# The first weight loads of a fused FFT filter and gated MLP: gate in quarters over two queues, up in halves

## The chip, the cores and the metric

The kernel runs on one core of one Trainium2 chip. The metric is the time of one execution on the device, in microseconds (us), median over several runs. A core has five engines that work side by side and meet through semaphores: TensorE (PE in the profile; its weight loads are PEld), VectorE (DVE), ScalarE (ACT), GpSimd (POOL) and SyncE (SP). Each takes its instructions in order. Transfers between main memory (HBM) and the core's memory (SBUF) are issued by one of these engines, as an instruction in its queue, and carried out by 16 DMA engines.

## The reference

Two branches work on the same normalized input, and both are added to the input. `A` filters the whole 2048 x 512 array by a two-dimensional FFT; `B` is a gated MLP with hidden width 1792.

```python
def _A_ref(x, w_r, w_i):
    X = rfft2(x.astype(float32), axes=(-2, -1))
    y = irfft2(X * (w_r + 1j * w_i), s=(S, D)).astype(bfloat16)
    return y

def _B_ref(x, w_gate, w_up, w_down):
    g = jnp.einsum("bsd,df->bsf", x, w_gate)
    u = jnp.einsum("bsd,df->bsf", x, w_up)
    h = _gelu(g) * u                      # tanh form
    return jnp.einsum("bsf,fd->bsd", h, w_down)

x = A_x                                   # 1 x 2048 x 512, bfloat16
xn = _layernorm(x, axis=-1)
return x + _A_ref(xn, A_w_r, A_w_i) + _B_ref(xn, B_w_gate, B_w_up, B_w_down)
```

## The kernel before

The 2048 rows are 16 chunks `c` of 128 rows (row 16p + c lies on partition p of chunk c). Everything is in bfloat16, with 32-bit sums in PSUM.

**Layer norm.** Of each chunk VectorE takes the statistics (L339, L342); the root of the variance comes from ScalarE for chunks 0 and 1 (L394) and from GpSimd for the others (L357, L361). The normalized chunk `xn` is needed with the contraction on the partitions: for chunks 0 to 3 TensorE transposes it (L351, four 128 x 128 transposes each) and a copy brings it to `xnT`, for chunks 4 to 15 a transposing DMA of SyncE does (L455).

**The MLP.** The contraction of 512 is four blocks `e` of 128 (`NE`), and the weight tiles `Wg_sb` and `Wu_sb` hold `[128, e, 1792]`. A unit of work (`unit`, L470) is a gate product into `g_ps`, an up product into `u_ps`, the GELU on ScalarE (`ge`, L503) and the product on VectorE (`hT`, L508). At first units are small: chunk 0 alone with the first 512 hidden columns, chunk 1 with the same columns, chunks 0 and 1 with columns 512 to 767 and 768 to 1023, then chunks 2 and 3; from hidden column 1024 on a unit takes four chunks. The gate product of the very first unit is cut in two (`mm_half`, L493): first all columns for e = 0 and 1, then for e = 2 and 3. All other products run column block by column block, each over all four e. Later come the down products (L817).

**The FFT.** It is matmuls with tables (`RF`, `CT`), folds on VectorE, a filter multiply and the way back, spread between the MLP's units. Three rows of indices, `idx_t`, serve the gathers of the filter (L594), which GpSimd issues from about 43 us on.

**What sets the order.** A small planner (`Plan`, L135) simulates five engines with estimated durations and writes out each engine's instructions in the order that results. It takes, in order of `key`, the operation that can start first. The arrival of loads is given to it as constants: `LAND` for x, `WG_LAND` and `WU_LAND` for the gate and up columns (L308 to L311), for example

```python
WG_LAND = [6.3] * 4 + [10.2] * 4 + [13.2] * 6
WU_LAND = [7.4] * 4 + [11.7] * 4 + [15.2] * 6
```

They shape the order alone; on the chip each instruction waits for its data. The order on each engine is fixed, so an operation whose data is late holds up all that stands behind it on its engine.

**The opening.** Ahead of the planned part stand the memsets (VectorE: `spin`, `eps_t`, `minus_half`), a warming square root on ScalarE (L280) that loads its table, 37 small matmuls on zeros (`spin`, L320) that keep TensorE at work until the first transposes, six more behind those (`spin_on`, L322), and all opening loads, in SyncE's queue, in the order of the code: x chunk 0, x chunk 1, the indices, gate and up columns 0 to 511, x 2 and 3, gate and up 512 to 1023, x 4 to 7, gate and up 1024 to 1791, x 8 to 11, `RF`, x 12 to 15, tables, filter. The loads' completions are counted on a ring of semaphores, and an issue that comes round to one still in use waits for it.

Of the kernel before, what the change touches and what calls it, by code (L numbers as in the profile page):

```python
# [10 lines left out]
P = 128  # L11
# [3 lines left out]
ALU = mybir.AluOpType  # L15
AF = mybir.ActivationFunctionType
# [3 lines left out]
NC = 16  # L20
NG = 8
NE = 4
DF = 1792
# [178 lines left out]
def kernel(  # L202
# [45 lines left out]
    def load_consts(first, last):  # L248
        a, b = ccols[first][0], sum(ccols[last])
        nc.sync.dma_start(out=CT[:, a:b], in_=cap[:, a:b])  # L250


    def load_x(c0, n, eng=nc.sync):
        eng.dma_start(out=x_t[:, c0:c0 + n, :], in_=x_v[:, c0:c0 + n, :])

    def load_w(a, b, eng=nc.sync):
        nc.sync.dma_start(out=Wg_sb[:, :, a:b], in_=wg_v[:, :, a:b])
        eng.dma_start(out=Wu_sb[:, :, a:b], in_=wu_v[:, :, a:b])
# [1 line left out]
    eps_t = pc.tile([P, 1], F32, name="eps_t")  # L260
    spin = pc.tile([P, P], BF16, name="spin")
    warm = pc.tile([P, 1], F32, name="warm")
    nc.vector.memset(spin[:], 0.0)
    nc.vector.memset(eps_t[:], EPS)
    minus_half = pc.tile([P, 4], F32, name="minus_half")
    nc.vector.memset(minus_half[:], -0.5)
    ident_t = pc.tile([P, P], BF16, name="ident_t")
    nc.gpsimd.memset(ident_t[:], 1.0)
    nc.gpsimd.affine_select(out=ident_t[:], in_=ident_t[:], pattern=[[-1, P]], compare_op=ALU.is_equal, fill=0.0,
                            base=0, channel_multiplier=1)  # L270

    def load_x(c0, n, eng=nc.sync):
        return eng.dma_start(out=x_t[:, c0:c0 + n, :], in_=x_v[:, c0:c0 + n, :])  # L273

# [1 line left out]
        v = wg_v if T is Wg_sb else wu_v  # L276
        return eng.dma_start(out=T[:, e, a:b], in_=v[:, e, a:b])  # L277

    pin = tc.keep_in_program_order
    pin(nc.scalar.activation(out=warm[:], in_=eps_t[:], func=AF.Sqrt, bias=eps_t[:], scale=1.0))  # L280
    pin(load_x(0, 1))
    pin(load_x(1, 1))
    idx_t = pc.tile([P, 3], I32, name="idx_t")
    nc.sync.dma_start(out=idx_t[:], in_=nc.inline_tensor(idx_np, name="spec_rows").ap())  # L284
    load_w(Wg_sb, 0, 512)
    load_w(Wu_sb, 0, 512)
    load_x(2, 2)
    load_w(Wg_sb, 512, 1024)
    load_w(Wu_sb, 512, 1024)
    load_x(4, 2)  # L290
    load_x(6, 2)
    load_w(Wg_sb, 1024, DF)
    load_w(Wu_sb, 1024, DF)
    load_x(8, 2)
    load_x(10, 2)
    for c in range(0, NC, 8):
        nc.sync.dma_start(out=RF_t[:, c:c + 8], in_=rf_d.rearrange("p (c k) -> p c k", c=NC)[:, c:c + 8])
    load_x(12, 2)
    load_x(14, 2)
    load_consts("F0", "L0")  # L300
    load_consts("I0", "M0")
    for T, w_in in ((TR, A_w_r), (TI, A_w_i)):
        rows = w_in.rearrange("(kb a h g) k -> h kb a (g k)", kb=NC, h=2, a=8)
        Tf = T.rearrange("p j k -> p (j k)")
        for h in range(2):
            nc.sync.dma_start(out=Tf[64 * h:64 * h + 64, W:8 * W], in_=rows[h, :, 0:4, W:8 * W])

    LAND = {0: 2.9, 1: 3.6, 2: 8.4, 3: 8.4}  # L308
    LAND.update({c: 11.5 if c < 8 else 17.5 if c < 12 else 20.5 for c in range(4, NC)})
    WG_LAND = [6.3] * 4 + [10.2] * 4 + [13.2] * 6  # L310
    WU_LAND = [7.4] * 4 + [11.7] * 4 + [15.2] * 6  # L311
    RF_LAND = 19.0

    ident = ident_t[:]
# [1 line left out]
    IQ = [cc(f"I{q}") for q in range(4)]  # L316

    sp_ps = ps.tile([P, D], F32, name="sp_ps", tag="S", bufs=4)
    for k in range(37):
        pin(nc.tensor.matmul(sp_ps[:, :P], lhsT=spin[:], rhs=spin[:], start=True, stop=True))  # L320

    def spin_on():  # L322
        for k in range(6):
            nc.tensor.matmul(sp_ps[:, :P], lhsT=spin[:], rhs=x_t[:, 0, :P], start=True, stop=True)
# [12 lines left out]
    def f_stats(c):  # L337
        tiles["st", c] = st = pw.tile([P, V.BN_STATS_DIM], F32, name="stats", bufs=4)
        V.bn_stats(out=st[:], in_=x_t[:, c, :])  # L339
# [34 lines left out]
    def first_two():  # L374
# [50 lines left out]
        o["copyt"].rel = ("S",)  # L425
        xT_op[1] = o["copyt"]
        xn_op[1] = o["xn1"]

    ROOT = 1.1
    first_two()  # L430

    def moments(c, key):
        s = add("DVE", 0.6, lambda: f_stats(c), key=key, t_min=LAND[c] if c < 4 else max(LAND[c], 14.7))
        return add("DVE", 0.1, lambda: f_mean(c), [s], key=key - 0.5)

    def second_two():
        m = [moments(c, -1200 + c) for c in (2, 3)]
        m = add("POOL", ROOT, lambda: root_eps(2, 2), m, key=-1190, lat=ROOT + 0.1)
        for c in (2, 3):
            xn_op[c] = add("DVE", 0.33, lambda c=c: f_norm_v(c, 0, D), [m], key=-1180 + c, lat=0.53)  # L440
            t = add("PE", 0.23, lambda c=c: f_T(c, 0, NE), [xn_op[c]], key=-880 + c, lat=0.5, acq=("S",))
            e, f = ("ACT", A.copy) if c == 2 else ("DVE", V.tensor_copy)
            xT_op[c] = add(e, 0.5, lambda c=c, f=f: f_Tc(c, 0, NE, f), [t], key=-1100 + c, rel=("S",))
# [26 lines left out]
    def unit(k, c0, n, f0, m=1):  # L470
# [50 lines left out]
            g = add("PE", occ / 2, lambda: mm_half(1), [xT_op[0], g], key=1000.1, lat=occ / 2 + 0.3)  # L521
        else:
            g = split("g_ps", "G", Wg_sb, 1000 + k, WG_LAND, m)
        u = split("u_ps", "U", Wu_sb, 1003.1 if k == 2 else 1000.5 + k, WU_LAND, (2, m, 1)[k] if k < 3 else m)
        ge = add("ACT", {1: 0.28, 2: 0.36, 4: 0.5}[n * m], f_ge, [g], key=-1000 + k,
                 lat={1: 0.38, 2: 0.48, 4: 0.7}[n * m], acq=("ge",), rel=("G",))
        h = add("DVE", {1: 0.21, 2: 0.34, 4: 0.61}[n * m], f_h, [ge, u], key=-1000 + k, rel=("U", "ge"))
# [318 lines left out]

    E_ = mybir.EngineType
    with tc.manual_schedule(engines={E_.PE, E_.DVE, E_.Activation, E_.Pool, E_.SP}):
        for op in plan.order():
            op.fn()  # L850

# [29 lines left out]
```

## Time and profile before

| | us |
|---|---|
| median of 6 runs | 178.6 (178.43 to 178.74) |
| the profiled execution | 179.56 |
| its span, first to last instruction | 177.9 (177.855) |
| TensorE busy | 172.5 |
| VectorE, ScalarE, GpSimd busy | 116.0, 95.9, 17.2 |
| first gate block: issued, landed | 2.17, 7.3 |
| first up block: issued, landed | 2.65, 8.75 |
| x chunks 2 and 3: issued, landed | 3.20, 9.5 |
| second gate block: issued, landed | 3.75, 10.95 |
| second up block: issued, landed | 4.22, 12.4 |

The profile is of one execution, which here was longer than each of the six runs. "Busy" is the time in which an engine had an instruction under way. A row of a timeline gives start, duration, engine, line and operation, the tile written and those read, and in brackets the idle time before it with what ended it. The chain of waits starts at the last instruction and goes back from each to what released it, so it shows what the end of the kernel hung on. In a row by windows, each engine's busy time in that stretch is followed by the granted TensorE clock (1.00 is full), the mean busy share of the DMA engines and the GB/s they moved.

### The profile page before, as it was taken

The numbers are of one execution on the slowest core, as the hardware profiler recorded it, in microseconds if no ns is written. First come the engines' busy times: TensorE is split into PE (matmuls) and PEld (weight loads), VectorE is DVE, ScalarE is ACT, GpSimd is POOL, SyncE is SP. The second block draws the span as 40 slices with busy tenths as digits, with TensorE's granted clock in tenths as the row PEclk, the third lists the DMA queues.
The fourth block names the chain that finished last, engine by engine and source line by source line (L and its number), as shares of the span: only waits on it lengthen the run. The fifth ranks groups of instructions, "written<-read, shape, count | busy, mean of one in ns | idle before, by whom it ended". The sixth has DMA issues, their size and how long they took to land.

```text
span 177.9 us, 3132 instructions
## 1 busy us (share of the span) xinstructions
PE 172.5 (97%) x1145; PEld 96.7 (54%) x1145; DVE 116.0 (65%) x255; ACT 95.9 (54%) x170; POOL 17.2 (10%) x38
## 2 busy tenths in 40 slices
PE   7699999999999999999999999999999999999993
PEld 7599845455545544555555445454444445444563
DVE  3487999987443598979899999634525334344233
ACT  4433398899735888898899974453112111211200
POOL 1020322504761000000000000000000000000000
PEclk9999999999999999999999999999999999999999
DMA  4999996424725902112201420200132222222212
GB/s 89 352 372 379 368 199 109 88 59 65 215 81 178 355 1 59 46 28 50 58 14 48 121 68 24 54 5 4 42 105 87 64 88 61 88 83 65 75 47 59
DMA packets 21871, 19.35 MB, mean 109 GB/s; under 512 B 8480, under 2 KB 20000, under 8 KB 21856
## 3 DMA queue, kind: packets, MB, share of 16 engines
q1 hardware_dynamic: 21440, 17.84, 35.1%
q0 software_dynamic: 416, 1.32, 2.5%
q8 instruction: 9, 0.15, 0.4%
q14 instruction: 6, 0.05, 0.1%
HBM read 13.38 MB, written 2.10 MB: 87 GB/s over the span
## 4 chain that ended last, share of the span: by engine, by line
PE 94%; DMA 3%; SPq 1%; issue 0%; DVE 0%
PE u_ps L490 27%; PE y_ps L817 27%; PE g_ps L490 27%; DMA Wu_sb<-in_B_w_up_dram 3%; PE gp L738 2%; PE bp L577 2%; PE yp L768 2%; PE dp L635 2%; PE y_ps L821 2%; PE ep L644 2%; SPq L273 0%; PE tp L351 0%; SPq L277 0%; SPq L284 0%; DVE y_sb L824 0%
## 5 line engine op out<-in xcount | busy, mean ns | idle before, releaser
L490 PE MATMUL u_ps<-xnT,Wu_sb 128*128 128x512 bf16 (+2 forms) x272 | 57.3, 341 | 0.2 <-DMA Wu_sb<-in_B_w_up_dram 0.2
L490 PE MATMUL g_ps<-xnT,Wg_sb 128*128 128x512 bf16 (+2 forms) x256 | 56.2, 349 | 0.0
L817 PE MATMUL y_ps<-Wd_sb,hT 128*128 128x512 bf16 (+2 forms) x252 | 51.1, 355 | 0.0
L508 DVE TENSOR_TENSOR hT<-u_ps,ge 128x512 bf16<-128x512 f32 x56 | 38.5, 688 | 18.2 <-PE u_ps L490 14.8
L503 ACT ACTIVATE ge<-g_ps 128x512 bf16<-128x512 f32 x56 | 33.7, 601 | 25.3 <-PE g_ps L490 21.4
L490 PEld LDWEIGHTS <-Wu_sb 128*128 128x128 bf16 x272 | 24.8, 98 | 21.0 <-DMA Wu_sb<-in_B_w_up_dram 0.3
L817 PEld LDWEIGHTS <-hT 128*128 128x128 bf16 x252 | 23.2, 98 | 22.4
L490 PEld LDWEIGHTS <-Wg_sb 128*128 128x128 bf16 x256 | 24.0, 98 | 20.6
L774 ACT CAST yf<-yp 128x512 bf16<-128x512 f32 x16 | 9.3, 586 | 40.5 <-PE yp L768 40.5
L824 DVE TENSOR_TENSOR y_sb<-y_ps,y_sb 128x512 bf16<-128x512 f32 (+2 forms) x18 | 11.1, 632 | 30.0 <-PE y_ps L821 30.0
L649 ACT CAST E<-ep 64x512 bf16<-64x512 f32 x32 | 18.5, 579 | 1.4 <-PE ep L644 1.0
L339 DVE BATCH_NORM_STATS2 stats<-x_t 128x6 f32<-128x512 bf16 x16 | 10.4, 674 | 2.4 <-DMA x_t<-in_A_x_dram 2.4
L452 ACT ACTIVATE xn<-x_t,nb,rstd 128x512 bf16<-128x512 bf16 x12 | 9.5, 811 | 1.0 <-POOL nb L370 1.0
L547 ACT CAST ds<-dp 128x512 bf16<-128x512 f32 x16 | 9.2, 597 | 0.8 <-PE dp L635 0.8
L547 ACT CAST Gs<-gp 128x512 bf16<-128x512 f32 x16 | 8.7, 591 | 0.6 <-PE gp L738 0.5
L547 ACT CAST Bs<-bp 128x512 bf16<-128x512 f32 x16 | 8.3, 607 | 0.5 <-PE bp L577 0.5
L780 DVE TENSOR_TENSOR lv<-yf 128x512 bf16<-128x512 bf16 x16 | 6.1, 421 | 1.5 <-ACT yf L774 0.6
L768 PEld LDWEIGHTS <-Gs 128*128 128x128 bf16 x64 | 4.8, 98 | 3.5
L787 DVE TENSOR_TENSOR yt<-lv 128x512 bf16<-128x512 bf16 x16 | 6.1, 422 | 0.3
L821 PE MATMUL y_ps<-yt,RI_t 128*128 128x512 bf16 (+2 forms) x18 | 6.1, 355 | 0.0
L768 PE MATMUL yp<-CT,Gs 128*128 128x128 bf16 x64 | 6.0, 219 | 0.0
L559 DVE TENSOR_TENSOR A<-xn 128x1024 bf16<-128x1024 bf16 x8 | 5.2, 676 | 1.0 <-ACT xn L452 1.0
(65 smaller groups left out, 119.2 us busy)
## 6 DMA issues: line engine op xcount, KB each, us to landing
F<-F SPq DMA_DIRECT2D x32, 64.0 KB, 2.0
y_sb<-in_A_x_dram SPq DMA_DIRECT2D x16, 128.0 KB, 2.1
out_dram<-y_sb SPq DMA_DIRECT2D x15, 128.0 KB, 1.7
x_t<-in_A_x_dram SPq DMA_DIRECT2D x7, 256.0 KB, 8.4
Wd_sb<-in_B_w_down_dram SPq DMA_DIRECT2D x1, 1792.0 KB, 7.8
Wg_sb<-in_B_w_gate_dram SPq DMA_DIRECT2D x2, 512.0 KB, 6.2
Wu_sb<-in_B_w_up_dram SPq DMA_DIRECT2D x2, 512.0 KB, 7.2
Wg_sb<-in_B_w_gate_dram SPq DMA_DIRECT2D x1, 768.0 KB, 9.0
```

The costliest lines, as they stand in the source:

```text
L339: V.bn_stats(out=st[:], in_=x_t[:, c, :])
L452: xn_op[c] = add("ACT", 0.72, lambda c=c: A.activation(out=xn[:, c, :], in_=x_t[:, c, :], func=AF.Identity, bias=nb[:, c:c + 1], scale=rst ...
L490: T_.matmul(b[name][:, f], lhsT=W_[:, e, (f0 + f) * P:(f0 + f + 1) * P], rhs=rhs[:, e, :], start=(e == 0), stop=(e == NE - 1))
L503: A.activation(out=b["ge"][:], in_=b["g_ps"][:], func=AF.Gelu_apprx_tanh)
L508: V.tensor_tensor(out=hT_of(sb, f0, m, o, w), in0=b["u_ps"][:], in1=b["ge"][:], op=ALU.mult)
L547: A.copy(out=o, in_=i)
L649: A.copy(out=b["E"][64 * h:64 * h + 64, r], in_=b["ep", h][64 * r:64 * r + 64])
L768: T_.matmul(t[:, q], lhsT=late["G"][:, q, c0 + j], rhs=IQ[q], start=(q == 0), stop=(q == 3), skip_group_check=True)
L774: A.copy(out=b["yf"][:, j], in_=b[j][:])
L817: T_.matmul(b[o][:], lhsT=hT_of(sb, f, 1, cl * P, P)[:, 0], rhs=Wd_sb[:, f, o:o + w], start=(f == 0), stop=False)
L821: T_.matmul(b[o][:], lhsT=late["RI"][:, c, :], rhs=late["yt"][:, c, o:o + w], start=False, stop=True)
L824: V.tensor_tensor(out=b["y"][:, o:o + w], in0=b[o][:], in1=b["y"][:, o:o + w], op=ALU.add)
```

## The change

The opening becomes a function that is called first inside the planned part, and its loads change:

- The first gate block (columns 0 to 511, 512 KB) is loaded as four DMAs, one for each e (128 x 512, 128 KB). e = 1 and 3 are issued by SyncE, e = 0 and 2 by ScalarE, behind its warming square root.
- VectorE writes zeros to the place of quarter e = 0 first, behind its three other memsets. The load of that quarter has to wait for this write.
- The first up block is loaded as two DMAs, e = 0 and 1, then e = 2 and 3, both from SyncE.
- The index load moves from behind x chunk 1 to behind x 12 to 15.
- x 4 to 7, 8 to 11 and 12 to 15 are one DMA each instead of two, and `RF` one instead of two.
- The planner's arrival times for the first and second gate and up blocks and for x chunks 2 and 3 are lower by 1.2 to 1.7.
- The statistics of chunks 2 and 3 may be planned only behind the copy of chunk 1's transposes (`after=chain_end`).
- The up product of the third unit loses its own late key (1003.1) and stands, as the others, just behind its gate product's (1002.5).

```diff
+    def opening():
+        nc.vector.memset(spin[:], 0.0)
+        nc.vector.memset(eps_t[:], EPS)
+        nc.vector.memset(minus_half[:], -0.5)
+        nc.vector.memset(Wg_sb[:, 0, 0:512], 0.0)
...
+        nc.scalar.activation(out=warm[:], in_=eps_t[:], func=AF.Sqrt, bias=eps_t[:], scale=1.0)
+        load_x(0, 1)
+        load_x(1, 1)
+        for e in range(NE):
+            load_w(Wg_sb, 0, 512, nc.sync if e % 2 else nc.scalar, e=e)
+        load_w(Wu_sb, 0, 512, e=slice(0, 2))
+        load_w(Wu_sb, 0, 512, e=slice(2, 4))
+        load_x(2, 2)
+        load_w(Wg_sb, 512, 1024)
+        load_w(Wu_sb, 512, 1024)
+        load_x(4, 4)
+        load_w(Wg_sb, 1024, DF)
+        load_w(Wu_sb, 1024, DF)
+        load_x(8, 4)
+        nc.sync.dma_start(out=RF_t[:], in_=rf_d.rearrange("p (c k) -> p c k", c=NC))
+        load_x(12, 4)
+        nc.sync.dma_start(out=idx_t[:], in_=nc.inline_tensor(idx_np, name="spec_rows").ap())
...
+        for k in range(37):
+            nc.tensor.matmul(sp_ps[:, :P], lhsT=spin[:], rhs=spin[:], start=True, stop=True)
+
-    LAND = {0: 2.9, 1: 3.6, 2: 8.4, 3: 8.4}
+    LAND = {0: 2.9, 1: 3.6, 2: 7.2, 3: 7.2}
...
-    WG_LAND = [6.3] * 4 + [10.2] * 4 + [13.2] * 6
-    WU_LAND = [7.4] * 4 + [11.7] * 4 + [15.2] * 6
+    WG_LAND = [5.0] * 4 + [8.6] * 4 + [13.2] * 6
+    WU_LAND = [6.2] * 4 + [10.0] * 4 + [15.2] * 6
...
-    first_two()
+    chain_end = first_two()
...
-        m = [moments(c, -1200 + c) for c in (2, 3)]
+        m = [moments(c, -1200 + c, chain_end) for c in (2, 3)]
...
-        u = split("u_ps", "U", Wu_sb, 1003.1 if k == 2 else 1000.5 + k, WU_LAND, (2, m, 1)[k] if k < 3 else m)
+        u = split("u_ps", "U", Wu_sb, 1000.5 + k, WU_LAND, (2, m, 1)[k] if k < 3 else m)
...
     with tc.manual_schedule(engines={E_.PE, E_.DVE, E_.Activation, E_.Pool, E_.SP}):
+        opening()
         for op in plan.order():
             op.fn()
```

## The prediction

> **What bounds the kernel now.** I read the page's busy shares first, then its chain of waits, then the first 14 us of TensorE's timeline, and last the rows on the loads.
>
> ```profile
> PE   7699999999999999999999999999999999999993
> ...
> PE 94%; DMA 3%; SPq 1%; issue 0%; DVE 0%
> ```
>
> Busy tenths of TensorE in 40 slices, and the chain's shares: after the first two slices TensorE never rests, and the chain runs through its matmuls. Only the head of the chain is something else:
>
> ```profile
> 1.71 0.42 SPq L284
> 2.13 0.04 issue
> 2.17 0.43 SPq L277
> 2.61 0.04 issue
> 2.65 6.10 DMA Wu_sb<-in_B_w_up_dram
> 8.75 0.05 issue
> 8.79 1.07 PE u_ps L490 x16
> ```
>
> The chain in order of time (start, us): the first up block, issued at 2.65, lands at 8.75, and everything afterwards hangs on the first up product at 8.79. TensorE in that stretch:
>
> ```profile
> 5.43 0.50 PE L324 MATMUL sp_ps<-x_t,spin 128*128 128x128 bf16 x6
> 7.34 1.07 PE L498 MATMUL g_ps<-xnT,Wg_sb 128*128 128x128 bf16 x16 [1.42 <-DMA Wg_sb<-in_B_w_gate_dram]
> 8.25 0.39 PE L351 MATMUL tp<-ident_t,xn 128*128 128x128 bf16 x4
> 8.79 1.07 PE L490 MATMUL u_ps<-xnT,Wu_sb 128*128 128x128 bf16 x16 [0.16 <-DMA Wu_sb<-in_B_w_up_dram]
> ```
>
> The brackets are the only two waits of TensorE behind its start. So a gain is what 8.79 falls by, as long as no new gap follows. How well the DMA engines worked before that (one row per us; the last two fields are DMA share and GB/s):
>
> ```profile
> 2.00:3.00 1.00, 1.00 (x12) 1.00 (x11) 0.00 (x1) 0.37 (x2) 0.00 (x0) 1.00 0.80 233
> 3.00:4.00 1.00, 1.00 (x12) 1.00 (x10) 0.96 (x3) 0.06 (x1) 0.00 (x0) 1.00 0.62 59
> 4.00:5.00 1.00, 1.00 (x13) 0.92 (x11) 0.96 (x5) 0.24 (x1) 0.00 (x0) 1.00 0.89 244
> ...
> 6.00:7.00 1.00, 0.00 (x0) 0.00 (x0) 0.30 (x1) 0.65 (x1) 0.00 (x0) 1.00 1.08 382
> ```
>
> Between 3 and 4 us they were 62% busy and moved 59 GB/s, against 382 later. The trace's packets show what sat there: the 128 packets of 12 B of the index load, from 2.75 to 3.5, and then, at 3.28 to 3.78, eleven 1 KB gate packets that took 0.34 to 0.97 us where the usual one takes 0.046. The first gate packet went out only behind those of the index load, at about 3.2.
>
> **The profiled execution against the median.** It took 179.56 us (span 177.86 and 1.70 around it), the six runs 178.6 at the median. I find the 0.96 in one packet: at 4.11 a gate packet took 1.48 us. The gate block's completion on the 16 DMA engines reads 5.61 to 6.26 for fourteen, then 6.73 and 7.30; the up block's is 7.74 on the fourteenth and 8.75 on the last. Without the late engines the up product would start at 7.78, 1.01 earlier: 178.55. So I take 7.78 as the ordinary run's start and 178.6 as its time, and rest the sum on that; that the profiled start were the ordinary one is a rival below.
>
> **The change part by part.**
>
> *The index load moves behind the x loads.* Taken out ahead of the gate block: one issue of 0.42 + 0.04 = 0.46 us on SP, and its 128 packets. The gate block's first issue goes from 2.17 to 1.71. Bounds on what all later landings gain: 0.46 (the issue slot alone), and, if the stalled packets went with it, the shortfall of the row 3:00 against the row 6:00, (382 - 59)/382 = 0.85 us, plus that of the row 4:00, (382 - 244)/382 = 0.36, together 1.2. The eleven stalls begin as the index packets end, but they are also the first gate packets, so I can't tell them apart; I take 0.7, nearer the low end, since the issue slot is certain and the stalls may stay. The gathers from 42.9 on are its only readers, some 20 us behind its new place. Free.
>
> The Trainium skill bears on this ("DMA: Bandwidth & Descriptors", Specifications): below 512 B a DMA engine does a read-modify-write. By it the 12 B rows would be the cause of the stalls and the gain the full 1.2; no row here separates that.
>
> *The first gate block in four DMAs of 128 KB.* Two per queue. A DMA of that size landed 2.2 us after its issue here (the two x loads). SP issues its two at 1.71 and 2.15; ACT's two wait for a memset. VectorE: the memset covers 128x256 words, the row for 128x64 is 0.11 us, so 0.11 to 0.44, beside an idle of 1.99 us before 3.00: nothing on the path. ACT's issues come at 1.3 (if they don't wait for the table load) or at 2.38, behind the table load and the warming activation (row 2.09 + 0.29). Behind them on ACT is the first root, at 3.94. Price per issue 0.42 to 1.43 us by SP's rows; the 1.43 stood behind three queued blocks, so I take 0.43: 2.38 + 0.9 = 3.3, before 3.94. The high end would end at 5.2 and push the root by 1.3. Landings: 2.38 + 2.2 = 4.6 and 5.0 if alone, and with the gate block's bytes at the row of 244 GB/s (0.52 MB, 2.1 us from 2.7) 4.9 to 5.4. The first product needs quarters 0 and 1 and the copies of the first chunk (5.43 + 0.29 and 5.71 + 0.27 on VectorE). Six spins at the matmul rate free TensorE at about 5.8. So the wait of 1.42 goes, the first product starts at 5.8, and late next is the x chain: x landed, statistics, root, normalization, transpose, copy.
>
> An early ACT quarter shares the engines with the second x load (landed 3.5, read at 3.82): 0 to 0.35 us later, of which 0.3 is slack. I take nothing; at worst 0.05.
>
> A rule speaks against this part: the skill's same page ("Rules for kernel authors") says that spreading DMAs over issuing engines brings no bandwidth, only issue time. Two slots of 0.43 on SP are then its whole worth; by it alone the sum would be that of the index load, 178.1.
>
> *The first up block in two DMAs.* One more issue of 0.43 on SP; both halves are needed at once, because each up group runs over all four quarters. So it lands as a whole: ordinary 7.74 less 0.46 to 1.2, that is 7.28 to 6.5, at my value 7.04. The up product can start at 5.8 + 0.91 (gate product, 7.34 to 8.25) + 0.23 (half of the eight transposes' 13.23 to 13.68) = 6.94 at best. So its start is 7.30 to 6.94, at my value 7.08: a gain of 0.48 to 0.84, mine 0.70.
>
> *Merged x and RF loads.* SP issues 22 DMAs where it issued 24. A load now waits for four chunks; the first chunk of 4 to 7 is read at 16.30, and the later half of them landed at 13.8. RF is read at 30.3. Free. SP's waits before re-used semaphores (the page of SP's waits has 1.8 us at most) begin two issues earlier, with over 1 MB queued: free.
>
> *The order of TensorE.* With the planner's new arrival times, worked by hand, the third up product moves from behind the transposes of chunks 2 and 3 and the fourth gate product to in front of them. Its slot: 7.08 + 0.91 + 0.89 + 0.89 + 0.87 = 10.64. It needs the second up block, which landed at 12.4 in the profiled execution, 11.4 without the two late engines, so 10.94 to 10.2, mine 10.7: a new wait of about 0.05 (0 to 0.1 in step with the above). The transposes then stand at 11.5; chunk 2 was normalized 3.3 us after its landing (9.47 to 12.75), which with an ordinary 8.4 less 0.7 is 11.0: 0.5 of cover.
>
> *What follows.* VectorE is full from 16 to 30, but its queue is moved whole. The end after the last matmul is untouched.
>
> Sum: 178.6 - 0.70 + 0.05 + 0.05 = **178.0 us**; by the profiled execution's own terms 179.56 - (8.79 - 7.08) + 0.1 = 177.95. Own range 177.75 to 178.25.
>
> **The rivals.** *The wait moves to the up block and nothing is won.* The same bytes come over the same engines; if the stalled packets belong to the gate weights and a second queue only interleaves, the up block lands at 7.6 to 7.8 and the time is 178.4 to 178.7. Against it: the 0.46 of the index slot.
>
> *The profiled start is the ordinary one.* Then 8.79 - 7.08 = 1.7 come off 178.6: 176.9 to 177.4. For it: the profiler may cost its 0.96 elsewhere. Against: the last two engines account for it almost exactly, and the planner's own arrival times (gate 6.3, up 7.4) fit the fourteen.
>
> *Slower: the third up product, moved forward, stalls.* It breaks even at a landing of the second up block of 7.78 + 3.56 = 11.34. A late engine like the profiled one puts it at 12.4 - 0.46 = 11.94, and the time at 178.6 + 0.6 = 179.2; before, this product stood 4.89 behind the first up product (13.68 - 8.79), now 3.56, and the load gains less than that on it. For it: one late engine stayed late to 24 us. Against: the six runs lie within 0.31 us.
>
> **How the numbers follow.** My forecast 62%, nothing won 14%, the large gain 10%, slower 14%. A measurement of this kernel tells about 0.2% (0.36 us) from no change. Three points of the forecast's 62 fall within that: faster 0.69, same 0.17, slower 0.14. The range for 8 in 10 leaves out the slower case and half of the large gain: 177.2 to 178.95.
>
> **What the profile would show.** Right: no wait of the first gate product on a DMA, its start at 5.8 to 6.0, the up product at 6.9 to 7.3, the row 3:00 well above 59 GB/s, no gap before 15 us. Wrong: a wait of the up product of over 0.3, a gap at the third up product, the first root later than 4.0.

## The result and the profile after

The changed kernel takes 179.39 us at the median of 17 runs, the kernel before 178.66 over 38 runs of the same comparison. The ratio is 1.0043, with a 95% interval of 1.0029 to 1.0057: slower by 0.73 us, where 178.0 was forecast and the range ended at 178.95. (Ratios and intervals here are estimated from the single runs, and can differ a little from the quotient of the two medians.)

The page of the changed kernel, busy tenths of TensorE in 40 slices and the shares of the chain:

```profile
PE   7889999999999999999999999999999999999993
...
PE 87%; DMA 6%; ACT 2%; DVE 2%; issue 1%; SPq 0%
```

TensorE still is the bound, but the share of DMA in the chain has doubled from 3% to 6%. The chain of waits in its first 14 us (start, us, what) shows where:

```profile
1.71 3.08 DMA Wg_sb<-in_B_w_gate_dram
4.79 0.02 issue
4.80 7.83 DMA Wu_sb<-in_B_w_up_dram
12.64 0.05 issue
12.68 1.05 PE u_ps L490 x8
```

Before, the chain left the loads at 8.75, with the first up block. Now it leaves them at 12.64, with the second up block, which is needed by the third up product. The same stretch on TensorE's timeline (in brackets the idle time and what ended it):

```profile
6.21 1.06 PE L498 MATMUL g_ps<-xnT,Wg_sb 128*128 128x128 bf16 x16
7.10 0.39 PE L350 MATMUL tp<-ident_t,xn 128*128 128x128 bf16 x4
7.33 0.28 PE L490 MATMUL u_ps<-xnT,Wu_sb 128*128 128x128 bf16 x2
8.04 0.95 PE L490 MATMUL u_ps<-xnT,Wu_sb 128*128 128x128 bf16 x14 [0.44 <-DMA Wu_sb<-in_B_w_up_dram]
...
11.22 1.05 PE L490 MATMUL g_ps<-xnT,Wg_sb 128*128 128x256 bf16 x8 [0.44 <-DMA Wg_sb<-in_B_w_gate_dram]
12.68 1.05 PE L490 MATMUL u_ps<-xnT,Wu_sb 128*128 128x256 bf16 x8 [0.42 <-DMA Wu_sb<-in_B_w_up_dram]
```

The wait of 1.42 before the first gate product is gone, and the first up product starts at 7.33 instead of 8.79. Then TensorE stops three times: inside the first up product, whose second half of the block is missing, before the third gate product, and before the third up product. Measured from start to start, over what the matmuls ahead need, these gaps are 0.60, 0.60 and 0.58 us, which is more than the 1.46 won. A fourth gap stands much later:

```profile
40.94 1.38 PE L577 MATMUL bp<-RF_t,xf 128*128 128x128 bf16 x16
```

Such a group takes 1.06 when nothing stops it; here four of its matmuls wait for a copy of ScalarE (`Bs`), and from its start to that of the next group it is 1.22 instead of 0.89, 0.33 more. The sum closes: 0.60 + 0.60 + 0.58 + 0.33 - 1.46 = 0.65, and the two profiled executions (180.22 and 179.56) lie 0.66 apart. Both stand above the medians of their runs, by 0.83 and 0.90, so a typical run of the change has less of the gaps; which of them, one profile can't tell.

What the DMA engines did, by windows of one us (each row: the window, its length, the busy time of TensorE, its weight loads, VectorE, ScalarE and GpSimd, then the granted clock, the DMA share and the GB/s):

```profile
3.00:4.00 1.00, 1.00 (x12) 1.00 (x10) 0.84 (x2) 0.09 (x1) 0.00 (x0) 1.00 1.03 286
4.00:5.00 1.00, 1.00 (x12) 0.91 (x9) 0.86 (x3) 0.21 (x1) 0.00 (x0) 1.00 0.92 311
...
6.00:7.00 1.00, 1.00 (x22) 1.00 (x20) 0.67 (x4) 0.96 (x1) 0.00 (x0) 1.00 0.84 283
7.00:8.00 1.00, 0.60 (x11) 0.42 (x8) 0.42 (x1) 0.60 (x1) 0.00 (x0) 1.00 0.82 214
```

The hole between 3 and 4 us is filled: 286 GB/s, 59 before. But the head start is given back at 6 to 8 us, 283 and 214 GB/s where there were 382 and 367 before. By 10 us both have moved about the same, 2.34 and 2.35 MB.

The mean hides the essential. A load is complete when the last of the 16 DMA engines has signalled, and the trace has these 16 completions. For the second half of the first up block they read 6.71 at the median engine and 7.99 at the last; for the second gate block 9.64 and 11.17, for the second up block 11.26 and 12.64. As an estimate from these times: with the median engine's, two of the three gaps would be gone (the first up product runs through from 7.33, the third gate product starts at 10.00), and the third up product, free at 10.87, would wait 0.4 for 11.26. One or a few engines are 1.3 to 1.5 us behind, and these loads land with them.

### The profile page after: what moved, and what is told of

Its sections match the earlier page's. It is cut to its first block, busy times and chain, and to the rows that moved or that the text cites. A ratio compares the mean times of both kernels' runs of the same rounds, so it can differ in the third digit from the quotient of the medians.

```text
span 178.5 us, 3132 instructions
## 1 busy us (share of the span) xinstructions
PE 173.2 (97%) x1145; PEld 96.8 (54%) x1145; DVE 116.2 (65%) x256; ACT 95.6 (54%) x170; POOL 17.6 (10%) x38
## 3 DMA queue, kind: packets, MB, share of 16 engines
q0 software_dynamic: 416, 1.32, 2.5%
## 4 chain that ended last, share of the span: by engine, by line
PE 87%; DMA 6%; ACT 2%; DVE 2%; issue 1%; SPq 0%
PE y_ps L817 27%; PE u_ps L490 25%; PE g_ps L490 24%; DMA Wu_sb<-in_B_w_up_dram 4%; PE gp L738 2%; PE yp L768 2%; PE dp L635 2%; PE y_ps L821 2%; PE ep L644 2%; DMA Wg_sb<-in_B_w_gate_dram 2%; PE bp L577 1%; ACT Bs L547 1%; DVE hT L508 1%; DVE A L559 1%; ACT ge L503 1%
## 5 line engine op out<-in xcount | busy, mean ns | idle before, releaser
L644 PE MATMUL ep<-ds,CT 128*128 128x512 bf16 x16 | 5.9, 379 | 0.0
## 6 DMA issues: line engine op xcount, KB each, us to landing
Wu_sb<-in_B_w_up_dram SPq DMA_DIRECT2D x1, 768.0 KB, 11.4
```

Of the source, the lines that this page charges most:

```text
L644: T_.matmul(t[:], lhsT=cc("L" if g + h else "L0"), rhs=b["ds", h][:], start=True, stop=True)
```

## The experiments

Three ideas were open: the second queue hurts; the cut into more DMAs hurts (through its address pattern, through the number of DMAs, or through the place on the semaphore ring); or the planner's new order and the merged loads hurt and the loads are fine. The runs come in four groups. Where the text says "index moved", it is the kernel before with nothing changed but the place of the index load. All times are medians; the kernel before took 178.62 to 178.71 beside them, and 178.95 beside one, the repeat of the index move. Costs "against the index move" compare with its 178.36. Up to 0.44 us of them stands not in the loads but at the end of the kernel, explained under "Why a cut costs".

### The change taken apart

**Loads alone.** The changed kernel with the old planner constants, keys and order:

```diff
-    WG_LAND = [5.0] * 4 + [8.6] * 4 + [13.2] * 6
-    WU_LAND = [6.2] * 4 + [10.0] * 4 + [15.2] * 6
+    WG_LAND = [6.3] * 4 + [10.2] * 4 + [13.2] * 6
+    WU_LAND = [7.4] * 4 + [11.7] * 4 + [15.2] * 6
...
-        u = split("u_ps", "U", Wu_sb, 1000.5 + k, WU_LAND, (2, m, 1)[k] if k < 3 else m)
+        u = split("u_ps", "U", Wu_sb, 1003.1 if k == 2 else 1000.5 + k, WU_LAND, (2, m, 1)[k] if k < 3 else m)
```

> The changed kernel's loads with the planner's old arrival times, the old key of the third up product and the statistics of chunks 2 and 3 free again: the loads without the new order. Theory A, the new order (third up product ahead of the transposes of chunks 2 and 3) stands too early for the second up block: the order is the loss, so this run falls back to 178.4 to 178.7 or better. Theory B, the split and re-queued loads make the 16 DMA engines slower between 6 and 8.5 us and the second blocks late: this run stays at 179.2 to 179.6, with the second gate block still landing at 11 us or later in the profile.

Measured: 179.08, ratio 1.0021 [1.0000, 1.0042]. Its TensorE timeline:

```profile
7.01 0.28 PE L490 MATMUL u_ps<-xnT,Wu_sb 128*128 128x128 bf16 x2
7.50 0.96 PE L490 MATMUL u_ps<-xnT,Wu_sb 128*128 128x128 bf16 x14 [0.22 <-DMA Wu_sb<-in_B_w_up_dram]
...
11.16 1.92 PE L490 MATMUL g_ps<-xnT,Wg_sb 128*128 128x256 bf16 x16 [0.91 <-DMA Wg_sb<-in_B_w_gate_dram]
```

Under the old order the up product starts earlier still, 1.78 before that in the profile of before, and most of this is lost at the third gate product (11.16, and 11.48 before): the second gate block completes at 8.95 on the median engine and at 11.11 on the last. So the loads alone don't win what they were counted for.

**Order alone.** The kernel before, its loads untouched, with the new arrival times, `after=chain_end` and the third up product's new key:

```diff
-    LAND = {0: 2.9, 1: 3.6, 2: 8.4, 3: 8.4}
+    LAND = {0: 2.9, 1: 3.6, 2: 7.2, 3: 7.2}
...
-        m = [moments(c, -1200 + c) for c in (2, 3)]
+        m = [moments(c, -1200 + c, chain_end) for c in (2, 3)]
...
-        u = split("u_ps", "U", Wu_sb, 1003.1 if k == 2 else 1000.5 + k, WU_LAND, (2, m, 1)[k] if k < 3 else m)
+        u = split("u_ps", "U", Wu_sb, 1000.5 + k, WU_LAND, (2, m, 1)[k] if k < 3 else m)
```

> The old opening and old loads, with the new arrival times, the new key and the new place of the statistics: the order without the loads. Theory A: the second up block lands as before (12.4 us in the profile, some 11.4 in ordinary runs) and the third up product waits for it, 179.0 to 179.6. Theory B: 178.5 to 178.8, no change.

Measured: 179.0, ratio 1.0014 [0.9993, 1.0035]. The third up product:

```profile
10.71 1.04 PE L491 MATMUL g_ps<-xnT,Wg_sb 128*128 128x256 bf16 x8
11.78 1.05 PE L491 MATMUL u_ps<-xnT,Wu_sb 128*128 128x256 bf16 x8
```

Behind a gate product at 10.71 it could start at 11.58; it starts at 11.78, just behind its block's landing at 11.74. The new order makes this product depend on the load, but by 0.2 us here; the interval does not tell its cost from nothing.

**Index load alone.**

```diff
-    nc.sync.dma_start(out=idx_t[:], in_=nc.inline_tensor(idx_np, name="spec_rows").ap())
     load_w(Wg_sb, 0, 512)
...
     load_x(14, 2)
+    nc.sync.dma_start(out=idx_t[:], in_=nc.inline_tensor(idx_np, name="spec_rows").ap())
     load_consts("F0", "L0")
```

> The kernel before with one edit: the index load moved from behind x chunk 1 to ahead of the first table load. My prediction's step says that the gate and up blocks land 0.46 to 1.2 us earlier and the time falls to 177.8 to 178.15. If the DMA engines lose the same time elsewhere, 178.5 to 178.8.

Measured: 178.36, ratio 0.9980 [0.9959, 1.0001]. The first up product starts at 7.59. What the index packets had been suspected of is still there; the window from 3 to 4 us:

```profile
3.00:4.00 1.00, 1.00 (x12) 1.00 (x10) 0.82 (x3) 0.00 (x0) 0.00 (x0) 1.00 0.76 122
```

With no index load near, seventeen 1 KB packets that start between 2.83 and 4.06 still take 0.2 to 1.0 us. So the index packets were not their cause. The interval touches 1, so the same kernel was measured again:

> The kernel before with nothing changed but the place of the index load, once more in more rounds, since 178.36 (ratio 0.998, interval 0.9959 to 1.0001) leaves open whether it is a gain. Theory "the issue slot of 0.46 in front of the first gate block is worth 0.3": 178.2 to 178.5, with the whole interval below 1. Theory "no difference, the earlier value was chance": 178.6 to 178.8.

Measured: 178.48 against 178.95, ratio 0.9976 [0.9965, 0.9987]: faster, by 0.47. No version tried is better, and both the kernel before and the changed one are slower. Its chain of waits (start, us, what) holds no DMA in the opening:

```profile
6.15 0.89 PE g_ps L498 x16
7.04 0.22 PE tp L351 x4
7.27 0.03 issue
7.30 1.07 PE u_ps L490 x16
8.37 0.89 PE g_ps L490 x16
```

TensorE goes from the warming matmuls to the end without waiting for a load. What is left to win in the opening lies in the x chain, not in the weights.

**Index moved and loads merged** (x 4 to 7, 8 to 11, 12 to 15 and `RF` as one DMA each):

```diff
-    load_x(4, 2)
-    load_x(6, 2)
+    load_x(4, 4)
...
-    load_x(8, 2)
-    load_x(10, 2)
+    load_x(8, 4)
-    for c in range(0, NC, 8):
-        nc.sync.dma_start(out=RF_t[:, c:c + 8], in_=rf_d.rearrange("p (c k) -> p c k", c=NC)[:, c:c + 8])
-    load_x(12, 2)
-    load_x(14, 2)
+    nc.sync.dma_start(out=RF_t[:], in_=rf_d.rearrange("p (c k) -> p c k", c=NC))
+    load_x(12, 4)
```

> The kernel before with the index load moved (the run that gave 178.36) and, new, the merged loads of x 4 to 7, 8 to 11, 12 to 15 and RF. Theory C, every piece of a weight block that starts while little is queued stalls the DMA engines: the merged loads start long after, no effect, 178.2 to 178.5. Rival D, the merged loads disturb: 178.7 or more.

Measured: 178.77, ratio 1.0004 [0.9991, 1.0016]. The gain of the index move is gone, so the merging costs about 0.4, and 0.24 of that is at the end of the kernel (see below). In the profiled execution, which at 179.28 was near the slowest of its runs, the first up product waits 0.69 for a block that lands at 7.96 (median engine 6.95), and a gap of 0.25 stands at 40.7. That a merged load issued behind the up block delays it is not shown.

**Index moved and up block in halves:**

```diff
-    load_w(Wu_sb, 0, 512)
+    load_w(Wu_sb, 0, 512, e=slice(0, 2))
+    load_w(Wu_sb, 0, 512, e=slice(2, 4))
```

> The kernel before with the index load moved and, new, the first up block in two DMAs. Theory C: one more start, the second up half and the second blocks land 0.2 to 0.6 later than in the run with the index load alone, 178.6 to 178.9. Rival (only the gate pieces or the second queue matter): 178.3 to 178.5.

Measured: 179.05, ratio 1.0025 [1.0010, 1.0040]: 0.7 more than with the index alone, and 0.44 of it at the end of the kernel.

**Index moved and gate block in quarters over both queues**, behind the VectorE write, as in the change:

```diff
-    load_w(Wg_sb, 0, 512)
+    nc.vector.memset(Wg_sb[:, 0, 0:512], 0.0)
+    for e in range(NE):
+        pin(load_w(Wg_sb, 0, 512, nc.sync if e % 2 else nc.scalar, e=e))
```

> The kernel before with the index load moved and, new, the first gate block in quarters over SyncE's and ScalarE's queues behind the memset; up block whole, old order. Theory C: the first gate product starts earlier (5.8 to 6.0), but the second gate block lands later than the 9.9 of the run with the index load alone, and the time is 178.7 to 179.1. Rival, my prediction's step: the up block lands at 7.0 and the time falls to 177.8 to 178.2.

Measured: 180.23, ratio 1.0087 [1.0065, 1.0109]: 1.9 more than with the index alone (0.33 of it at the end of the kernel), and by itself worse than the whole change.

```profile
6.30 1.06 PE L500 MATMUL g_ps<-xnT,Wg_sb 128*128 128x128 bf16 x16
8.74 1.07 PE L492 MATMUL u_ps<-xnT,Wu_sb 128*128 128x128 bf16 x16 [1.16 <-DMA Wu_sb<-in_B_w_up_dram]
```

The gate weights are there in time; the uncut up block behind them completes at 6.85 on the median engine and at 8.69 on the last. The parts don't add: 0.7 + 1.9 + 0.4 on top of the index move would be 181.4, and all new loads together (the first run above) took 179.08. About 1.0 of that difference is the end of the kernel, 0.44 + 0.33 + 0.24, which comes with the number of DMAs: the merges take away as many as the cuts add.

### Which queue

Two variants of the changed kernel: all four quarters from SyncE, and the gate block whole from SyncE.

```diff
-            load_w(Wg_sb, 0, 512, nc.sync if e % 2 else nc.scalar, e=e)
+            load_w(Wg_sb, 0, 512, e=e)
```

> The changed kernel with all four gate quarters issued by SyncE; ScalarE issues none. If the second queue is what slows the loads (theory B by way of the queue), 178.5 to 178.9 and the gap between 6 and 8.5 us in the moved bytes closes; under theory A, or theory B by way of the splitting itself, it stays within 0.2 of 179.4.

Measured: 180.55, ratio 1.0105 [1.0071, 1.0138]. Without the second queue the change is worse, by 1.2. Here all 16 engines are late, not one: the up block completes at 7.80 on the median engine and at 8.54 on the last.

```diff
-        for e in range(NE):
-            load_w(Wg_sb, 0, 512, nc.sync if e % 2 else nc.scalar, e=e)
+        load_w(Wg_sb, 0, 512)
```

> The changed kernel with the first gate block again as one DMA of SyncE; up halves, merged loads, moved index load and new order stay. If the gate's four pieces are the part of the loads that costs, it falls from 179.4 to 178.7 to 179.0 (the order's 0.35 stays). If the up halves or the merged loads cost, it stays above 179.1.

Measured: 179.81, ratio 1.0061 [1.0040, 1.0083]. With the gate block whole again, but the up block still in halves, the first gate product waits 0.80 for a block that lands at 5.56 on the median engine and 6.79 on the last. In this run 0.18 more stands at the end of the kernel. Both runs speak against the second queue as the cause. The next one does so directly: index moved, and the whole gate block issued by ScalarE behind the VectorE write.

```diff
-    load_w(Wg_sb, 0, 512)
+    nc.vector.memset(Wg_sb[:, 0, 0:512], 0.0)
+    pin(load_w(Wg_sb, 0, 512, nc.scalar))
```

> The kernel before with the index load moved and, new, the first gate block whole but issued by ScalarE behind a VectorE memset. If a second queue alone costs nothing: the gate block is issued at 1.32 and the up block at 1.71, 0.4 earlier, and the time is 178.0 to 178.4. If the second queue disturbs: 178.7 or more.

Measured: 178.50, ratio 0.9981 [0.9960, 1.0003].

```profile
6.25 1.21 PE L499 MATMUL g_ps<-xnT,Wg_sb 128*128 128x128 bf16 x16
7.52 1.06 PE L491 MATMUL u_ps<-xnT,Wu_sb 128*128 128x128 bf16 x16
```

No wait for a load, and this execution too has the gap near 40 us. Second queue, VectorE write and DMA issues on ScalarE show no cost together, and they bring nothing over SyncE's queue either.

### What about the cut

All of these have the index moved and the gate block on SyncE's queue, first in four DMAs by e, then in four by partitions, then in two by e.

```diff
-    load_w(Wg_sb, 0, 512)
+    for e in range(NE):
+        load_w(Wg_sb, 0, 512, e=e)
```

> The kernel before with the index load moved and, new, the first gate block in four DMAs of SyncE cut by e, up block whole, no second queue, no memset. If the cut is the cost and the second queue has no part in it, as slow as the quarters over two queues (180.23): 179.8 to 180.7. If the second queue is the cost: 178.3 to 178.8.

Measured: 179.93, ratio 1.0057 [1.0036, 1.0078]. Timeline, then one window of this run and below it the same window of the index move:

```profile
5.81 1.06 PE L499 MATMUL g_ps<-xnT,Wg_sb 128*128 128x128 bf16 x16
8.87 1.07 PE L491 MATMUL u_ps<-xnT,Wu_sb 128*128 128x128 bf16 x16 [1.79 <-DMA Wu_sb<-in_B_w_up_dram]
```

```profile
5.00:6.00 1.00, 1.00 (x16) 0.80 (x15) 0.84 (x6) 0.90 (x2) 0.00 (x0) 1.00 0.69 119
...
5.00:6.00 1.00, 1.00 (x12) 0.58 (x10) 0.83 (x6) 0.78 (x2) 0.00 (x0) 1.00 1.08 384
```

Here the mechanism is visible in the mean too. The gate product starts at 5.81, as the prediction had it, and between 5 and 6 us, in the middle of the up block, the engines move 119 GB/s; the kernel with only the index moved has 384. The up product pays 1.79.

```diff
-    load_w(Wg_sb, 0, 512)
+    for i in range(0, P, 32):
+        nc.sync.dma_start(out=Wg_sb[i:i + 32, :, 0:512], in_=wg_v[i:i + 32, :, 0:512])
```

> The kernel before with the index load moved (178.36) and, new, the first gate block in four DMAs of SyncE cut by partitions (32 each, all four e), so that each DMA still reads rows of all four e. Theory N, the number of weight DMAs at the start costs (more starts, more completions): as slow as the cut by e, 179.5 or more. Theory E, it is the cut by e that costs, because then all 16 DMA engines read one stretch of 128 neighbouring rows: 178.3 to 178.8.

Measured: 180.06, ratio 1.0083 [1.0053, 1.0113]. Here the delay appears one block later, at the third gate product:

```profile
11.71 1.92 PE L491 MATMUL g_ps<-xnT,Wg_sb 128*128 128x256 bf16 x16 [0.84 <-DMA Wg_sb<-in_B_w_gate_dram]
```

Cut by partitions, each DMA keeps the address pattern of the whole block for its rows, and it costs the same. So the pattern by e is not what hurts. The Trainium skill has a rule for such a cut ("DMA: Bandwidth & Descriptors", Rules for kernel authors): don't split a transfer into parts by partitions, since all of them go over the same 16 engines; use one of 128 partitions. The run agrees and is harsher: it isn't just useless, it costs 1.7 us against 178.36, of which 0.33 is at the end of the kernel.

```diff
-    load_w(Wg_sb, 0, 512)
+    load_w(Wg_sb, 0, 512, e=slice(0, 2))
+    load_w(Wg_sb, 0, 512, e=slice(2, 4))
```

> The kernel before with the index load moved and, new, the first gate block in two DMAs of SyncE, e 0 and 1, then 2 and 3. If the cost grows with the cut: between 178.4 and the quarters, some 179.0, as the up halves (179.05). If only pieces of a single e cost: 178.2 to 178.5.

Measured: 180.08, ratio 1.0069 [1.0048, 1.0091]. One DMA more already costs all of it, 1.7; four pieces are no worse than two. In the profiled execution these 1.7 are 0.94 in the opening, 0.31 at the gap near 40 us and 0.44 at the end of the kernel.

```profile
8.06 1.07 PE L491 MATMUL u_ps<-xnT,Wu_sb 128*128 128x128 bf16 x16 [0.27 <-DMA Wu_sb<-in_B_w_up_dram]
...
11.21 1.92 PE L491 MATMUL g_ps<-xnT,Wg_sb 128*128 128x256 bf16 x16 [0.29 <-DMA Wg_sb<-in_B_w_gate_dram]
```

### Why a cut costs

Four more runs, to tell apart the number of DMAs ahead, the place on the ring of semaphores, the queue, and the first weight load as such. First, the cut moved to the second gate block (index moved, first blocks whole):

```diff
-    load_w(Wg_sb, 512, 1024)
+    load_w(Wg_sb, 512, 1024, e=slice(0, 2))
+    load_w(Wg_sb, 512, 1024, e=slice(2, 4))
```

> The kernel with only the index load moved (178.36), and its second gate block (columns 512 to 1023) cut in two DMAs by e. The first gate block whole: 178.36; cut in two: 180.08. Theory "any cut among the loads of the first microseconds costs": 179.5 to 180.1, with packets of 0.2 to 1.2 us behind the cut and the second gate and up blocks 1 us later than 9.87 and 11.35. Theory "only the first weight load is sensitive, as it goes out while the first rows of the weights are read": 178.2 to 178.6, as without the cut.

Measured: 178.98, ratio 1.0010 [0.9994, 1.0027], between the two expectations: some 0.6 more than the index move alone, and 0.43 of it at the end of the kernel. In its profile a late engine holds up x chunks 2 and 3 (7.73 at the median engine, 9.01 at the last), which stand ahead of the cut block in the queue, and all behind them; the opening is 0.28 longer in this one execution. What is left of the cost beside the end is too small to tell from nothing.

Second, halves of the first gate block with x chunks 0 and 1 in one DMA, so that all later loads keep their number, ring place and issue time:

```diff
-    pin(load_x(0, 1))
-    pin(load_x(1, 1))
+    pin(load_x(0, 2))
```

> The first gate block in two DMAs by e as in the run at 180.08, but x chunks 0 and 1 in one DMA instead of two, so that every load from the up block on has the same number in SyncE's queue, the same place on the ring of semaphores and the same issue time as in the kernel at 178.36. Theory "the number of DMAs ahead, or the place on the ring": up block lands at about 7.5 and the second up block at about 11.4; time 178.4 plus up to 0.3 for the later x chunk 0. Theory "the size of the gate pieces, wherever they stand": up block at 8.0, second up block at 12.6, 179.8 to 180.3.

Measured: 179.93, ratio 1.0065 [1.0040, 1.0090]. The later x chunk makes this run hard to read by its time: it lands at 4.19, and the first transpose waits 1.03 for it. The landings tell: the up block completes at 6.45 on the median engine and at 8.32 on the last, the second up block at 12.71, not at 11.4. The count of DMAs ahead, or the place on the ring, is not the cause of the late landings.

Third, halves of the first gate block and x chunks 4 to 7 merged, so that the count is as before from the third gate block on:

```diff
-    load_w(Wg_sb, 0, 512)
+    load_w(Wg_sb, 0, 512, e=slice(0, 2))
+    load_w(Wg_sb, 0, 512, e=slice(2, 4))
...
-    load_x(4, 2)
-    load_x(6, 2)
+    load_x(4, 4)
```

> The first gate block in two DMAs by e as in the run at 180.08, and x chunks 4 to 7 in one DMA instead of two, so that the DMA count, and the ring of semaphores, is as in the kernel at 178.36 from the third gate block on. Theory "what costs is behind the eighth DMA, where issues wait": 178.4 to 178.9. Theory "the cost is made in the first 9 us" (the up block at 8.0, the second up block at 12.6): 179.8 to 180.3.

Measured: 179.8, ratio 1.0057 [1.0038, 1.0075], the second up block at 12.86 (median engine 11.42). The late landings are made before the ring comes round.

Fourth, the halves both on ScalarE's queue, with SyncE's uncut:

```diff
-    load_w(Wg_sb, 0, 512)
+    nc.vector.memset(Wg_sb[:, 0, 0:512], 0.0)
+    pin(load_w(Wg_sb, 0, 512, nc.scalar, e=slice(0, 2)))
+    pin(load_w(Wg_sb, 0, 512, nc.scalar, e=slice(2, 4)))
```

> The first gate block in two DMAs by e, both issued by ScalarE behind a VectorE write, so that SyncE's queue has one DMA less than in the kernel at 178.36 (as the kernel with the whole block on ScalarE, at 178.50, has). Theory "one more DMA on SyncE's queue shifts all behind it": 178.3 to 178.7, up block at 7.4. Theory "pieces of 256 KB cost on whichever queue": 179.8 to 180.3, with late DMA engines behind them.

Measured: 179.3, ratio 1.0037 [1.0014, 1.0060], again between the two. But the landings are those of the uncut kernel: up block 7.25 (median engine 6.94), second up block 11.35 (10.84). There is no late engine, and the opening loses little:

```profile
7.11 0.62 PE L500 MATMUL g_ps<-xnT,Wg_sb 128*128 128x128 bf16 x8 [0.37 <-DMA Wg_sb<-in_B_w_gate_dram]
```

The x chunk 1 lands at 4.14 (3.5 without the second queue), and the second gate half only at 7.07, beside SyncE's up block at 7.25. The first up product then starts at 7.79, only 0.20 behind the index move's 7.59. Of the 0.9 that this run is longer, the rest is 0.31 at the gap near 40 us and 0.44 at the end of the kernel.

**The end of the kernel.** The DMAs of SyncE and ScalarE are counted on a ring of eight semaphores, and behind the last store SyncE waits for all eight, one after the other in the ring's order, about 0.065 us each in the traces. The last VectorE addition of the index move, and of the gate block in halves on SyncE's queue:

```profile
173.91 0.29 DVE L824 TENSOR_TENSOR y_sb<-y_ps,y_sb 128x128 bf16<-128x128 f32 x1 [0.55 <-PE y_ps L821]
...
175.16 0.29 DVE L825 TENSOR_TENSOR y_sb<-y_ps,y_sb 128x128 bf16<-128x128 f32 x1 [0.55 <-PE y_ps L822]
```

The addition ends at 174.20 and the span at 176.65, 2.45 later; with the halves it ends at 175.45 and the span at 178.34, 2.89 later. The last store lands 1.5 behind the addition in both. With 104 DMAs, as in the kernel before, that store has the last of the eight semaphores, and SyncE has gone through the other seven while it lands. With 105 it has the first, and the other seven waits follow. All traces agree: this end takes 2.45 with 104 DMAs, 2.89 with 105, 2.77 with 107, 2.62 with 101 and 2.69 with 100. So a DMA more or less, wherever it stands, costs up to 0.44 here. The change itself has 104 again and pays nothing.

The completions in the profiled executions side by side (us; last of the 16 engines / median engine), and where each is longer than the profiled index move of 178.38: in the opening (the start of the product at 39.39 us there), at the gap behind that product, and at the end. Between these places the executions differ by less than 0.01.

| weight loads | median | profiled | first up block | second up block | opening | gap | end |
|---|---|---|---|---|---|---|---|
| kernel before | 178.66 | 179.56 | 8.75 / 7.48 | 12.47 / 11.25 | 1.21 | 0 | 0 |
| the same, new order | 179.0 | 178.99 | 7.97 / 7.44 | 11.74 / 11.20 | 0.64 | 0 | 0 |
| index moved, all whole | 178.36 | 178.38 | 7.54 / 7.02 | 11.35 / 10.81 | 0 | 0 | 0 |
| the same, again | 178.48 | 178.07 | 7.25 / 7.04 | 11.27 / 10.89 | -0.29 | 0.01 | 0 |
| index moved, x and `RF` merged | 178.77 | 179.28 | 7.96 / 6.95 | 11.60 / 10.83 | 0.42 | 0.25 | 0.24 |
| gate whole, on ScalarE | 178.50 | 178.58 | 7.41 / 6.92 | 11.24 / 10.87 | -0.08 | 0.31 | 0 |
| gate in 2, on ScalarE | 179.30 | 179.30 | 7.25 / 6.94 | 11.35 / 10.84 | 0.20 | 0.31 | 0.44 |
| second gate block in 2 | 178.98 | 179.06 | 7.16 / 6.90 | 12.17 / 10.88 | 0.28 | 0 | 0.43 |
| up in 2 | 179.05 | 178.94 | 7.67 / 6.99 | 11.86 / 11.04 | 0.15 | 0 | 0.44 |
| gate in 2 | 180.08 | 180.04 | 8.02 / 6.85 | 12.64 / 11.35 | 0.94 | 0.31 | 0.44 |
| gate in 2, x 0 and 1 merged | 179.93 | 179.34 | 8.32 / 6.45 | 12.71 / 10.95 | 0.99 | 0 | 0 |
| gate in 2, x 4 to 7 merged | 179.8 | 179.52 | 8.01 / 7.37 | 12.86 / 11.42 | 1.17 | 0 | 0 |
| gate in 4 by e | 179.93 | 179.97 | 8.83 / 7.51 | 12.41 / 11.59 | 1.29 | 0 | 0.33 |
| gate in 4 by partitions | 180.06 | 180.12 | 7.97 / 7.43 | 13.14 / 11.48 | 1.44 | 0 | 0.33 |
| gate in 4, two queues | 180.23 | 180.26 | 8.69 / 6.85 | 12.95 / 11.12 | 1.24 | 0.32 | 0.33 |
| all new loads, old order | 179.08 | 179.55 | 7.46 / 6.68 | 12.57 / 10.44 | 0.89 | 0.31 | 0 |
| the change | 179.39 | 180.22 | 7.99 / 6.71 | 12.64 / 11.26 | 1.54 | 0.33 | 0 |
| the change, gate whole | 179.81 | 179.51 | 8.13 / 7.03 | 11.73 / 11.03 | 0.64 | 0.31 | 0.18 |
| the change, gate in 4 on SyncE | 180.55 | 180.16 | 8.54 / 7.80 | 12.59 / 11.94 | 1.50 | 0.31 | 0 |

(In the run with x 4 to 7 merged one execution of eight took 648 us; without it the median is 179.75.)

What this shows: a cut of the first gate block makes the opening 0.94 to 1.44 longer than the index move when all its pieces, or every other one, stand in SyncE's queue, in all six executions that have it with the up block whole. Behind a cut in SyncE's queue stand packets of 0.5 us and more between 4.5 and 11.5 us (2 to 13 of them, the longest 0.53 to 1.25; 0.046 is usual for 1 KB, 0.09 for 2 KB), and in ten of the twelve such executions one or a few DMA engines are 1.1 to 2.1 us behind the median one on the first or the second up block. With the index moved and the weights whole, or the gate cut in ScalarE's queue, no packet of that stretch reaches 0.5 and the last engine is 0.2 to 0.6 behind; the merged loads are the exception (three such packets, up to 1.0 behind). The gap near 40 us comes with and without cuts; what brings it is not shown. Cuts of the up block or of the second gate block lengthened the opening by 0.15 and 0.28, no more than whole blocks differ among themselves (-0.29 to 0.42).

What it does not show: what in the DMA system makes these packets long. Address pattern, number of DMAs ahead and second queue are out, and so is the place on the ring, which costs at the end of the kernel alone. One candidate from the Trainium skill ("DMA: Bandwidth & Descriptors", Queues, rings and completion order): an engine's semaphore write for a DMA lands only after all of that engine's earlier writes, across its queues. By it, each DMA more would add such a point per engine. No run here shows it, and the run with halves on ScalarE, which has as many of those points, speaks against it as the whole story. That stays open. So does the late engine of the kernel before's own profiled execution, which had no cut: such engines occur without one, too. Later in the kernel all 19 executions have one: a 16 KB packet of an instruction queue, at 11.6 to 13.0 us, takes 1.1 us, and on the third gate block the last engine is 1.3 to 2.9 behind the median one. Where the weights are whole nothing waits for it there.

## Why the prediction was wrong

**The profiled execution stands 0.96 above the ordinary one, for one late engine: right in the main.** Kernels with whole weight blocks have their first up product at 7.30 to 8.02 and medians of 178.36 to 179.0; the median of before stayed at 178.66. The old loads in another execution, the run with the new order alone, gave 8.02, 0.77 before 8.79, where the prediction had 7.78. The rival that took 8.79 for ordinary is out.

**The index load, 0.7: right in kind, too large.** It is 0.29 in the first measurement and 0.47 in the second, better resolved one (0.23 to 0.63 by its interval), which fits the issue slot of 0.46. The bound of 1.2 needed the stalled packets to go with the index packets, and they stayed. So the reading that took the Trainium skill's rule ("DMA: Bandwidth & Descriptors", Specifications: below 512 B a DMA engine does a read-modify-write) for the cause of the stalls, and with it 1.2 us, is out; the rule itself no run here tests.

**Gate in quarters, first gate product at 5.8: nearly right, 6.21.** The wait of 1.42 went. ScalarE issued at 1.32, beside its table load, the early end of the bounds; so its quarters met the second x chunk, which landed at 4.08 instead of 3.5. That was priced at 0 to 0.35 with 0.3 of slack, and was 0.6.

**The up block lands at 7.04 and the product starts at 7.08: this is the step that failed.** It took the ordinary landing of the uncut block, 7.74, less what the index move gives, and priced the cuts themselves at one issue slot each; no run stood behind that price. The median engine did land at 6.71. The last landed at 7.99, and a block counts with its last engine, so the product that was to start at 7.08 and run through started at 7.33 and stopped until 8.04. The second gate and up blocks, behind it in the queue, were late in the same way: the third up product started at 12.68 where the sum had 10.7. These 2.0 us and the 0.33 near 41 us, less 0.05 that the sum had set aside for another wait, are the miss in the profiled execution, 180.22 against 177.95. Alone, the cut of the gate block makes the opening 0.94 to 1.44 longer (the whole run 1.6 to 1.9).

**Merged loads, free: wrong by about 0.4 when alone**, of which 0.24 is the end of the kernel, where a DMA count of 100 instead of 104 leaves more waits behind the last store. The sum had no term for the count. In the change it costs nothing, since cuts and merges make 104 again; the rest of the 0.4 has no cause shown.

**The new order, a wait of 0.05: mis-sized, and the rival on it was half right.** The slower rival broke even at a landing of the second up block of 11.34; it came at 12.64, and by the rival's arithmetic that costs 1.3. The third gate and the third up product lost 1.18 together, half of it at the gate product, which neither the forecast nor a rival had. But the rival let a chance engine do it, at 14%, and behind a cut such engines are common. Its time, 179.2, comes close to the 179.39 measured, and that is partly luck. The order alone took 179.0, which is not told from no change. One reading behind the 0.05 was off by itself: without the two late engines the second up block of the profiled execution completes at 11.54, not 11.4, which makes the forecast wait 0.2.

**A second queue brings only issue time (the Trainium skill, "DMA: Bandwidth & Descriptors", Rules for kernel authors): borne out.** The whole gate block on ScalarE took 178.50, on SyncE 178.36 and 178.48. The rule that spoke against the change, by which the index load was its whole worth, was right on the second queue and on what there was to win; the harm of the cuts was not in it.

**The range** was built from rivals that moved a wait from one place to the next and held the transfer's own speed fixed, and it left out the one slower rival. It had no case in which a cut makes the loads behind it later, and so ended at 178.95.

## What to carry to other kernels

Here each load was as late as the slowest of the 16 DMA engines. Compare the last and the median completion of each load before you count on a mean rate, and price a cut of an opening load from both sides, below nothing too, as long as no run shows it free; here one cut of the first gate block cost 1.7 us, more than the wait of 1.42 that it was to take away. Before you put the cost of an added DMA down to its transfer, look at the end of the kernel too: 0.44 of those 1.7 is there, by the DMA count alone. Try the smallest part of a change alone: the best version moved one small load, and the cuts beside it hid that gain.

## What was not expected of the hardware

- The first 1 KB packets of the first weight load take up to 1.0 us, and the rate falls to 122 GB/s from 3 to 4 us (346 in the next), also with no small load near.
- In the one profiled execution with the second gate block cut, an engine is late on a load that stands ahead of it in the queue.
- ScalarE issued two DMAs (0.86 us for both, from 1.32) while its table load ran from 0.80 to 2.08.
- Costs of load changes were far from additive: 0.7, 1.9 and 0.4 alone, 0.7 together; 1.0 of the difference is the end of the kernel.
- The end of the kernel took 2.45 to 2.89 us, by which of the eight semaphores the last store fell on.
